# A retention layer and a gated MLP on one core: the same 937 jobs in another order on every engine

## The chip, the cores and the metric

The kernel runs on one core of one Trainium2 chip. The metric is the device time of one execution in microseconds; the time before is the median of three runs. A core has five instruction streams that run on their own and meet at semaphores: PE (TensorE, matrix products, with PEld for its weight loads), DVE (VectorE), ACT (ScalarE), POOL (GpSimd) and SP (SyncE, which here only issues transfers). Each stream is worked off strictly in the order in which it was written. Transfers run on 16 DMA engines that all of SP's queue shares.

## The reference

Inputs are q, k, v of 8 batches x 8 heads x 576 rows x 64, in float32, and the weights of a gated MLP.

```python
scores = scale * q @ k^T                       # per batch and head
ret    = scores * gamma_h ** (t - s), s <= t   # decay, causal
x      = ret @ v, heads side by side           # (8, 576, 512)
h      = gelu(x @ w_in);  u, v = halves of h   # 2 x 512
v_n    = (v - mean) / sqrt(var + 1e-6) * g_ln
v_s    = w_sg @ v_n (over the 576 rows) + b_sg
out    = x + (u * v_s) @ w_out
```

## The kernel before

**Tiles.** Two batches make a pair of 1152 rows, so nine tiles of 128 rows; there are four pairs and 36 tiles (`i` = 0 to 35). The retention of a pair is worked in five blocks `b` (20 in all): blocks 0, 1, 3, 4 of a pair have 256 rows, the one in the middle has 64 rows of each of the two batches. Within a block the causal products are made directly; what came before is carried as a running sum of k^T v ("Z").

**A block's jobs.** SP loads q, k and v (`a_load`, L348; 512 KB each, or q of two blocks at once; the middle block in two transfers of 128 KB each, L351). `a_prep` casts them to bf16 on DVE, ACT or POOL, q and v with the decay multiplied in (L391), k as a plain copy (by the helper `move`, L264 for ACT, L265 for DVE and POOL). PE transposes k and q (`a_Tp` L446, `a_T` L428; blocks 15 and 18 by DMA transpose, `a_TX` L471), and their results are evacuated (`a_Tpev`, `a_Tev`). PE forms the scores (`a_S`, L502), DVE masks them (`a_Sev`, L515, L518), PE forms k^T v (`a_Z`, L538), DVE adds it up (L563, L566) and it is cast (`a_Zev`). PE forms the block's output (`a_O`, `a_O2`, L584), which is evacuated into xT (`a_Oev`).

**A tile's jobs.** V half of the input product (`m_V`, L652), gelu (`m_Vg`, ACT, L659), statistics (`m_stats`, DVE, L667, L668), 1/sqrt (`m_rs`, four POOL instructions, L672 to L675), norm (`m_norm`, ACT, L684, L687); U half (`m_U`, L699) and gelu (`m_Ug`, L709). When a batch's tiles are normalised, eight W products mix its rows (`m_W`, L718: five matmuls each, named by (batch, column block, row half)) and DVE multiplies each with u (`m_Wg`, L728). The output product (`m_O`, L749) is added to x by DVE (`m_Oev`, L766); for tiles from 9 on x comes as a DMA transpose of xT (`m_X`, L758), and `m_store` (L771) writes the tile.

**Weights.** w_in comes in two transfers of 1 MB (V half first, then U half), w_sg in three (L292 twice, L296), w_out in one; each is cast on the way. w_sg is transposed on PE into wT (`build_wT`, L819), evacuated, and shifted by two transfers for the second batch of a pair. Small products turn g_ln and b_sg into columns and rows.

**What sets the order.** Every piece of work is a `Job` with a default engine and, for many, a choice of others (`alt`). Jobs are numbered in the order in which the kernel's loops create them, 0 to 936. The string `ORDER` lists all numbers once; a letter behind a number sets its engine (D, A or P for DVE, ACT, POOL). The kernel emits the jobs in that order, so the string sets at once the sequence on each engine, the engine of the movable jobs, the rotation of the buffers (eight `ld`, three `vb`, two `pp` and four `d` of PSUM, five `xr`, and so on) and what waits for what. The times in the `Job` calls play no part in it.

```python
def follow(self, order):
    for x in order.split():
        if x[0] == "f":
            j = self.fill(int(x[1:]), ...)
        else:
            j = self.jobs[int(x.rstrip("DAP"))]
            if not x.isdigit():
                j.eng = {"D": "DVE", "A": "ACT", "P": "POOL"}[x[-1]]
        self.done.append(j)
```

`fill` puts warm-up matmuls on zeros before the first real work: `f2` one of 256 columns, `f1` one of 128.

Job numbers that are spoken of below:

| number | job |
|---|---|
| 0, 1, 2 | loads of q, k, v of block 0 |
| 3, 9 | loads of w_in, V half and U half; 4, 5 and 10, 11 their casts |
| 12, 13, 14 | loads of q, k, v of block 2; 23 is q of block 3 |
| 15, 16, 17 | loads of w_sg; 18 to 22 their casts |
| 102, 104 | PE transposes of k and q of block 0; 103, 105 their evacuations |
| 108 | cast of v of block 1; 297 is the Z product of block 1 |
| 132, 133, 136 | casts of q of block 5 and its transposes on PE |
| 315, 330, 331 | m_rs of tiles 2 and 4, norm of tile 4 |
| 333 | the first W product |
| 59, 62, 64 | loads of v of blocks 14, 15, 16; 179, 185 the casts of the first two |
| 63, 187 | load and cast of k of block 16; 69 the load of k of block 18 |
| 65, 66, 67 | loads of q, k, v of block 17 |
| 576, 578 | DMA transpose and evacuation of tile 13; 577 its product |
| 585, 586, 587 | output product, evacuation and store of tile 14 |
| 926, 930 | DMA transposes of tiles 34 and 35; 928 is tile 34's evacuation |

Of the kernel before, what the change touches and what calls it, by code (L numbers as in the profile page):

```python
# [20 lines left out]
    '0 f2 1 2 6 7 99D 83D 3 100A 102 8 73 103D 101P 104 74 105A 9 106P 17 203 77 204 12 205 84P 107A 275 206 75 '  # L21
    '277A 109 76D 78D 111 110D 85P 280 112A 5P 281 4A 282D 207 276 283A 278 15 284 108P 208 13 209 285 16 279A 286 '
    '297 287 298 210 11A 10P 14 300 299A 290 23 288 22A 113P 289 301 291 294 80A 302 292 303D 304A 24 18D 305 293 '
    '114D 19A 311 306 313 25 295 307 20P 296 116 79P 308 31 117D 314 21P 115P 211 309 89 212 312 32 310 93 321 94A '
    '118D 322 318 90A 95 324A 33 87 319 315 119A 323D 96D 325 320D 86A 88D 121 34 326 123 120P 328 122A 327 316 '
    '124D 37 329 330 361 215 317 213 362 216 91 35 125P 331 92D 214 333 335 26 363P 126A 127P 366 336 334 128 364 '
    '367 130 368D 369A 339 332 129D 341 131D 365A 350 39 340 219 132P 342 383 217 220 370 36 348 351 371 133P 384 '
    '373 218 337 38 372 134P 136 349 385 137D 138A 386 343 374 387A 140 40 375 81A 389 344 388A 380 141D 98 28 395 '
    '390 338 29 221 223 41 381 222 378 135P 396 376 224 379 30 392 139P 391 97 377 227 27 44 433 397 434 435A 393 '
    '228 142P 382 438 455 436 398 225 143P 394 439 42 352 440A 45 456 441A 399 458 355 437A 226 442 144P 400 356D '  # L30
    '145 353A 43 445 146D 457A 443 448 446 444 401 357 450 150D 412 451 229 447 449 459 417 230 452 408 413 354 418 '
    '410 409 46 147P 479 460 476 480 461D 419 482A 47 453 481D 463 411 454 148P 420 483 478D 464 477 462A 427 82A '
    '149D 466 465 428A 153P 484 429 151 467 485 50 523 155 152D 469 48 156A 154P 486 524 526 402 468 470 488 233 '
    '487 231 234 406 52 404 473 403 235 232 49 345 157P 475 236 358 525A 405 528 359A 407 158D 237 346A 545 529 490 '
    '347 414 238 58 159P 530A 51 471 489 163D 531A 421 415D 472 474 546 161 527D 54 422A 165 162D 532 360 166D 535 '
    '424 60 536 160D 533 547 425A 534 600 56 241 548 537 538 550A 53 602A 601 540 549A 542 242 539 55 557 541 603 '
    '167P 243 558 239 551 240 544 164P 430 552 244 543 57 491 169P 431A 493 554 494 492 61 605 553 555 174P 622 245 '
    '59 606 556 604P 499 607A 507 623 608A 561 625 609 178A 508 500 615 624A 246 168P 610 497 616 64 611 626 562 '
    '172P 498 170 563 627 643 171D 612 628A 515 629D 645A 173P 564 613 559 565 644 416 247 560 175P 511 180 501 '
    '181A 630 423 502 182P 248 503 495 614 631 176 426 632 617 584 183P 496 568 618 63 177D 638 432 67 184P 509 569 '  # L40
    '639 646 510 619 251 62 690 252 647 580 648A 649A 504 691 620 581 692P 516 65 693 179P 505 187A 253 517 249 633 '
# [1087 lines left out]
```

## Time and profile before

| | |
|---|---|
| time before, median of 3 runs | 211.9 us (211.15 to 212.1) |
| the profiled execution, its own time | 212.94 us |
| its span | 211.2 us |
| busy: PE, DVE, ACT, POOL | 187.3, 160.3, 120.5, 101.4 us |
| moved by DMA | 49.04 MB, mean 232 GB/s |
| mean granted clock of PE | 0.992 |

Times in the profile are microseconds from the start of the span. A line of a timeline gives the start, the duration, the engine, the line of the kernel, the operation and its tiles, the count of instructions merged into it, and in brackets the idle time just before it on that engine, with what ended it. A line of stages gives the stretch, its length, then busy time and count of instructions for each engine, the granted clock of PE, the DMA engines' mean busy share and the GB/s moved. PE's ends are modelled, so a busy PE is not PE at its peak. The clock column counts as full any time for which the trace has no record, as before 20.5 us here.

### The profile page before, as it was taken

The numbers are of one execution on the slowest core, as the hardware profiler recorded it, in microseconds if no ns is written. First come the engines' busy times: TensorE is split into PE (matmuls) and PEld (weight loads), VectorE is DVE, ScalarE is ACT, GpSimd is POOL, SyncE is SP. The second block draws the span as 40 slices with busy tenths as digits, with TensorE's granted clock in tenths as the row PEclk, the third lists the DMA queues.
The fourth block names the chain that finished last, engine by engine and source line by source line (L and its number), as shares of the span: only waits on it lengthen the run. The fifth ranks groups of instructions, "written<-read, shape, count | busy, mean of one in ns | idle before, by whom it ended". The sixth has DMA issues, their size and how long they took to land.

```text
span 211.2 us, 7761 instructions
## 1 busy us (share of the span) xinstructions
PE 187.3 (89%) x3313; PEld 127.4 (60%) x3341; DVE 160.3 (76%) x312; ACT 120.5 (57%) x196; POOL 101.4 (48%) x157
## 2 busy tenths in 40 slices
PE   2288787799799999999999988799999999999992
PEld 0265454576575757657667746477567666656661
DVE  5576757799698879998886858897787699665673
ACT  5246695944788386667596444766636653255300
POOL 8266547876664696405689746244236071022000
PEclk9999997999999999999999999999999999999999
DMA  5999999999999999799999699999698966147875
GB/s 163 290 341 281 234 206 291 301 300 291 234 197 289 276 318 257 171 247 334 269 287 227 180 280 159 231 211 180 221 303 157 216 187 202 53 108 204 165 219 204
DMA packets 87109, 49.04 MB, mean 232 GB/s; under 512 B 37082, under 2 KB 80354, under 8 KB 87074
## 3 DMA queue, kind: packets, MB, share of 16 engines
q1 hardware_dynamic: 87056, 48.53, 95.3%
q8 instruction: 26, 0.43, 0.9%
q14 instruction: 9, 0.07, 0.1%
q10 hardware_dynamic: 18, 0.00, 0.0%
HBM read 32.79 MB, written 9.44 MB: 200 GB/s over the span
## 4 chain that ended last, share of the span: by engine, by line
PE 68%; DMA 11%; DVE 6%; SPq 5%; ACT 4%; issue 3%; POOL 2%; DVEq 0%; POOLq 0%
PE wp L718 17%; PE hv L652 12%; PE op L749 12%; PE hu L699 11%; PE pp L584 6%; DMA ld<-in_k_dram 6%; PE pp L502 4%; DMA ld<-in_q_dram 4%; SPq L351 3%; PE pp L428 2%; PE zp L538 2%; DVE ret L515 2%; ACT qT L264 1%; DMA xr<-xT 1%; PE pp L446 1%
## 5 line engine op out<-in xcount | busy, mean ns | idle before, releaser
L515 DVE TENSOR_TENSOR ret<-pp,msk 128x1024 bf16<-128x1024 f32 x32 | 38.6, 1217 | 4.5 <-PE pp L502 4.4
L718 PE MATMUL wp<-wT,vn 128*128 128x288 bf16 x256 | 41.1, 286 | 0.8 <-DVE wT L265 0.8
L699 PE MATMUL hu<-xT,w_in 128*128 128x256 bf16 (+1 forms) x320 | 36.2, 262 | 2.2 <-POOL w_in L265 1.4
L652 PE MATMUL hv<-w_in,xT 128*128 128x512 bf16 x127 | 36.0, 391 | 1.6 <-issue 0.4
L667 DVE BATCH_NORM_STATS2 bst<-vg 128x6 f32<-128x512 f32 x36 | 24.7, 685 | 13.9 <-ACT vg L659 13.9
L749 PE MATMUL op<-w_out,uT 128*128 128x512 bf16 (+1 forms) x137 | 34.4, 373 | 0.8 <-DVE uT L728 0.2
L699 PEld LDWEIGHTS <-w_in 128*128 128x128 bf16 x320 | 28.1, 98 | 9.0 <-POOL w_in L265 1.9
L728 DVE TENSOR_TENSOR uT<-wp,uT 128x288 bf16<-128x288 f32 x64 | 27.5, 448 | 6.8 <-PE wp L718 6.2
L672 POOL TENSOR_SCALAR mv<-mv 128x2 f32<-128x2 f32 (+1 forms) x20 | 5.4, 271 | 56.0 <-DVE mv L668 43.3
L391 POOL TENSOR_TENSOR vb<-ld,gpow 128x1024 bf16<-128x1024 f32 (+1 forms) x16 | 27.8, 1743 | 9.3 <-DMA ld<-in_v_dram 9.2
L687 ACT ACTIVATE vn<-vg,mv 128x512 bf16<-128x512 f32 x32 | 25.3, 807 | 10.3 <-POOL mv L675 10.3
L709 ACT ACTIVATE uT<-hu 128x512 bf16<-128x512 f32 x36 | 20.9, 594 | 15.8 <-PE hu L699 15.7
L718 PEld LDWEIGHTS <-vn 128*128 128x128 bf16 x256 | 24.2, 98 | 9.5 <-ACT vmid L684 1.0
L659 ACT ACTIVATE vg<-hv 128x512 f32<-128x512 f32 x36 | 21.0, 593 | 11.5 <-PE hv L652 5.8
L264 ACT ACTIVATE xT<-pp 128x512 bf16<-128x512 f32 (+1 forms) x31 | 16.6, 566 | 18.3 <-PE pp L584 15.0
L391 POOL TENSOR_TENSOR qb<-ldq,gpow 128x1024 bf16<-128x1024 f32 x11 | 20.7, 1904 | 9.2 <-DMA ldq<-in_q_dram 7.9
L766 DVE TENSOR_TENSOR ob<-op,xr 128x512 f32<-128x512 f32 (+1 forms) x28 | 18.5, 668 | 6.3 <-PE op L749 6.0
L652 PEld LDWEIGHTS <-xT 128*128 128x128 bf16 x144 | 13.5, 100 | 13.4 <-issue 1.3
L749 PEld LDWEIGHTS <-uT 128*128 128x128 bf16 x148 | 14.0, 98 | 11.9 <-issue 0.4
L718 PE MATMUL wp<-wT,vmid 128*128 128x288 bf16 x64 | 18.0, 287 | 0.0
L673 POOL TENSOR_TENSOR mv<-mv,mhalf 128x2 f32<-128x2 f32 (+1 forms) x20 | 13.8, 690 | 1.7
L584 PE MATMUL pp<-qT,zb 64*64 64x128 bf16 (+1 forms) x256 | 12.2, 225 | 1.5 <-issue 1.0
(115 smaller groups left out, 253.6 us busy)
## 6 DMA issues: line engine op xcount, KB each, us to landing
out_dram<-ob SPq DMA_DIRECT2D x35, 256.0 KB, 2.8
ld<-in_k_dram SPq DMA_DIRECT2D x16, 512.0 KB, 6.6
ld<-in_v_dram SPq DMA_DIRECT2D x16, 512.0 KB, 6.8
ldq<-in_q_dram SPq DMA_DIRECT2D x6, 1024.0 KB, 7.7
ld<-in_q_dram SPq DMA_DIRECT2D x4, 512.0 KB, 7.4
xT<-in_moe_w_sg_dram SPq DMA_DIRECT2D x2, 576.0 KB, 8.5
xT<-in_moe_w_in_dram SPq DMA_DIRECT2D x1, 1024.0 KB, 8.3
uT<-in_moe_w_in_dram SPq DMA_DIRECT2D x1, 1024.0 KB
```

The lines of the kernel that those rows point to most:

```text
L391: ve.tensor_tensor(dst, src, g.unsqueeze(len(src.shape) - 1).to_broadcast(list(src.shape)), op=Alu.mult)
L515: ins = nc.vector.tensor_tensor(ret[:].rearrange("p r (k t) -> p (r k) t", k=2), sc[:].rearrange("p r (k t) -> p (r k) t", k=2), (msk2 if ...
L584: nc.tensor.matmul(ot[64 * c:64 * c + 64, bank, j * cs:(j + 1) * cs], lhsT, rhs, start=(bank, c) not in begun, stop=True, skip_group_check ...
L652: ins = nc.tensor.matmul(hv[:], xTs[p][:, m, kk, :], w_in[:, kk, F2:], start=(kk == 0), stop=(kk == KK - 1))
L659: unfence(nc.scalar.activation(vgs[i][:], cur.pop(("hv", i))[:], Act.Gelu_apprx_tanh), ("V", i))
L667: nc.vector.bn_stats(bst[:], vgs[i][:])
L687: nc.scalar.activation(vn[:], vg[:], Act.Identity, scale=mv[:, s, 2:3], bias=mv[:, s, 3:4])
L699: ins = nc.tensor.matmul(hu[:, n, :], w_in[:, kk, 128 * c:128 * c + 128], xTs[p][:, m:m + w, kk, :], start=(kk == 0), stop=(kk == KK - 1), ...
L709: unfence(nc.scalar.activation(uTs[p][:, c0:c1, 128 * m:128 * m + 128 * w], cur.pop(("hu", i, half))[:], Act.Gelu_apprx_tanh), ("U", i, half))
L718: ins = nc.tensor.matmul(ps[:], vns[t0 + j][e][:, 128 * c:128 * c + 128], wT[e][:, j, half * HS:(half + 1) * HS], start=(j == 0), stop=(j ...
L728: ins = nc.vector.tensor_tensor(uTs[p][:, c, col:col + HS], cur.pop(("wp", b, c, half))[:], uTs[p][:, c, col:col + HS], op=Alu.mult)
L749: ins = nc.tensor.matmul(op[:], uTs[p][:, c, r], w_out[:, c, cs], start=(p >= XP and c == 0), stop=(c == KK - 1), skip_group_check=True)
```

## The change

The string `ORDER` is replaced; nothing else differs. The new one holds the same job numbers, `f1` in place of `f2`, other engine letters on 79 jobs, and other positions for most jobs. A job moves by four places on PE on average, by 26 at most. The first 44 PE jobs are the same set in both, and so are the first 190. On SP the load of v of block 0 now comes ahead of that of k, q of block 2 ahead of the U half of w_in, and k, v of block 2 and q of block 3 ahead of w_sg. Of the engines' jobs, 28 go from ACT or DVE to POOL, 15 from POOL to ACT or DVE, 19 from DVE to ACT and 17 from ACT to DVE.

The diff, cut to the lines that hold the head, the places named in the prediction, and the end:

```diff
-    '0 f2 1 2 6 7 99D 83D 3 100A 102 8 73 103D 101P 104 74 105A 9 106P 17 203 77 204 12 205 84P 107A 275 206 75 '
-    '277A 109 76D 78D 111 110D 85P 280 112A 5P 281 4A 282D 207 276 283A 278 15 284 108P 208 13 209 285 16 279A 286 '
-    '297 287 298 210 11A 10P 14 300 299A 290 23 288 22A 113P 289 301 291 294 80A 302 292 303D 304A 24 18D 305 293 '
-    '114D 19A 311 306 313 25 295 307 20P 296 116 79P 308 31 117D 314 21P 115P 211 309 89 212 312 32 310 93 321 94A '
...
-    '172P 498 170 563 627 643 171D 612 628A 515 629D 645A 173P 564 613 559 565 644 416 247 560 175P 511 180 501 '
-    '181A 630 423 502 182P 248 503 495 614 631 176 426 632 617 584 183P 496 568 618 63 177D 638 432 67 184P 509 569 '
-    '639 646 510 619 251 62 690 252 647 580 648A 649A 504 691 620 581 692P 516 65 693 179P 505 187A 253 517 249 633 '
...
-    '847 892 926 872 855 897 744 848 873 849 900 745 904 856 901 902 918 905 898 903 746 850 899 922 914 851 911 '
-    '915 852 906 912 916 907 913 908 917 930 919 909 923 920 931 921 924 934 927 925 935 932 936 928 933 929 '
+    '0 f1 2 1 6 7 99D 73 74 3 101P 8 83P 100A 102 12 104 103D 275 106P 105A 77 276 277A 203 78A 9 75 204 107A 85P '
+    '205 13 206 76A 109 111 112A 278 280 110D 79A 281 5D 282A 4P 283A 14 108D 23 297 113D 209 284 298 300 299P 210 '
+    '207 279P 285 287 81P 208 288 286 17 301 11P 15 289 302 16 10P 24 114A 304A 294 116 25 290 117D 303D 292 291 '
+    '115P 295 31 211 305 212 118P 321 306 308 293 307 311 19A 18P 309 22D 322 318 296 313 310 32 20P 312 323D 314 '
...
+    '540 498 552 553 55 493 541 69 243 168A 494 239 622 543 538 623 244 61 554 539 625 544 495 240 555 430 63 174A '
...
+    '511 180 184A 508 617 614 503 187P 499 618 181D 509 175P 177A 630 500 510 580 619 631 62 646 581 690 251 647 '
+    '691 59 570 648A 252 519 182P 620 512 621 693 426 633 571 632 504 183P 634 513 649A 636 694A 635 249 186 253 '
...
+    '565 255 642 767 712 769D 696 585 697A 768 713 698A 770 699 656 586 256 702 658 703 520 700 587 659 657 65 '
+    '572 521 676 701 66 714 573 257 518 704 715 660 717A 506 677 716A 707 596 709 661 258 705 708 588 197P 710 261 '
...
+    '848 930 833 898 834 849 753 872 754 854 873 899 902 855 904 903 856 900 905 918 850 901 911 851 914 852 912 '
+    '916 913 908 917 922 915 906 909 919 926 907 931 920 934 932 923 921 935 933 927 924 936 925 928 929 '
```

## The prediction

> **What bounds the kernel now.** I read the page first, for the busy shares and the forty slices. Columns of the slices: one digit for 5.3 us, in tenths.
>
> ```profile
> span 211.2 us, 7761 instructions
> PE 187.3 (89%) x3313; PEld 127.4 (60%) x3341; DVE 160.3 (76%) x312; ACT 120.5 (57%) x196; POOL 101.4 (48%) x157
> ...
> PE   2288787799799999999999988799999999999992
> ...
> PEclk9999997999999999999999999999999999999999
> DMA  5999999999999999799999699999698966147875
> ```
>
> TensorE (PE) is busy 187.3 of 211.2 us. Its weak slices are the first eight, two near 125 us and the last; the DMA engines are as full as it until 165 us. Next I cut the span into stages (us; then busy us and count of PE, weight loads, DVE, ACT, POOL; granted clock, DMA share, GB/s).
>
> ```profile
> 0.00:9.00 9.00, 1.77 (x19) 0.96 (x19) 4.69 (x23) 4.21 (x5) 4.45 (x26) 1.00 0.85 215
> 9.00:21.00 12.00, 9.57 (x234) 6.92 (x233) 8.61 (x20) 5.82 (x8) 7.87 (x6) 1.00 1.15 309
> 21.00:42.00 21.00, 15.86 (x297) 10.65 (x299) 14.07 (x29) 16.19 (x27) 13.43 (x20) 0.92 1.13 257
> 42.00:60.00 18.00, 16.53 (x356) 11.59 (x362) 15.73 (x25) 11.02 (x19) 10.88 (x11) 1.00 1.11 266
> 60.00:113.00 53.00, 52.31 (x1140) 36.49 (x1144) 44.83 (x78) 37.22 (x65) 33.40 (x43) 1.00 1.04 268
> 113.00:134.00 21.00, 18.35 (x368) 12.82 (x364) 14.93 (x29) 10.56 (x18) 13.50 (x19) 1.00 1.04 205
> 134.00:200.00 66.00, 65.53 (x883) 43.62 (x892) 51.26 (x99) 35.50 (x59) 17.90 (x34) 1.00 0.81 186
> ```
>
> From 60 to 113 and from 134 to 200 us PE idles 0.69 and 0.47 us: an order can give little there and lose much. What can be won lies before 42 us (14.8 us idle), in 42 to 60 (1.5), in 113 to 134 (2.65) and in the last 4 us.
>
> The head, in order of time:
>
> ```profile
> 7.34 1.06 ACT L264 ACTIVATE qb<-ld 128x1024 bf16<-128x1024 f32 x1 [1.77 <-DMA ld<-in_k_dram]
> 8.45 0.45 PEld L446 LDWEIGHTS <-qb 64*128 64x128 bf16 x16 [6.71 <-ACT qb L264]
> ...
> 9.85 0.61 PE L446 MATMUL pp<-ident,qb 64*128 64x64 bf16 x16 [0.58 <-DVE qT L265]
> ...
> 11.57 0.64 PE L502 MATMUL pp<-qT 64*64 64x128 bf16 x16 [1.11 <-ACT qT L264]
> ```
>
> PE's first real work waits for k of block 0 and its cast; then each step waits for the one before. The third view is the clock, in three neighbouring stretches of 3.4 us:
>
> ```profile
> 27.35:30.76 3.41, 3.36 (x53) 2.10 (x50) 1.79 (x4) 3.22 (x6) 0.51 (x2) 1.00 1.25 204
> 30.76:34.17 3.41, 1.46 (x38) 1.01 (x40) 2.21 (x4) 1.68 (x4) 3.19 (x5) 1.00 0.94 250
> 34.17:37.59 3.42, 3.20 (x39) 1.95 (x36) 2.21 (x6) 2.29 (x5) 2.38 (x5) 0.50 1.17 300
> ```
>
> A stretch in which PE was busy 1.46 of 3.41 us is followed by one at half clock. Last, the dip at 124 to 133 us:
>
> ```profile
> 124.48 1.06 ACT L264 ACTIVATE kb<-ld 128x1024 bf16<-128x1024 f32 x1 [3.09 <-DMA ld<-in_k_dram]
> ...
> 126.77 1.05 PE L699 MATMUL hu<-xT,w_in 128*128 128x128 bf16 x16 [0.74 <-ACT vg L659]
> ...
> 129.41 1.90 POOL L391 TENSOR_TENSOR vb<-ld,gpow 128x1024 bf16<-128x1024 f32 x1
> ...
> 131.37 0.63 PE L538 MATMUL zp<-vb,kb 64*64 64x64 bf16 x44 [0.50 <-POOL vb L391]
> ...
> 133.14 0.25 PE L584 MATMUL pp<-qT,zb 64*64 64x128 bf16 x4 [1.02 <-issue]
> ```
>
> ACT stands 3.09 us for k of block 16, behind it the norm and the gelu that free PE's buffer; the statistics come late, POOL's v cast with them, and PE waits 0.74 and 0.50 us. The 1.02 us are "issue", for which the profile shows no releaser.
>
> **The change, part by part.** It is measured against this execution: 211.2 us of span and 1.7 around it, 212.94, which is 1.04 above the median of 211.9.
>
> *Engines.* 79 jobs change engine. Each at the mean of its kind on its new engine (v cast 1.90 us on POOL, 1.22 on DVE; k cast 1.06 ACT, 1.04 POOL; block evacuation 0.60 ACT, 0.69 DVE): DVE loses 3 us, ACT 4, POOL gains 11. POOL then is at 54%, so this alone is hidden; where a moved job stands behind a late one, it counts below.
>
> *Head to PE's 44th job, the first W product* (both orders hold the same jobs up to there). Loads of 512 KB land every 1.82 us: k of block 0 at 7.32, v at 9.13. After, v is issued first, so k lands at 9.13 and ACT is done at 10.2: 1.8 us later. The two groups of 16 transposes now stand together ahead of the first evacuation, so the 0.58 us wait goes and DVE (0.69) and ACT (1.02) evacuate side by side: scores at 12.6 instead of 11.57. Output of block 0: ACT's casts for block 1 come after one row copy, PE starts it at 16.0 instead of 15.24. Then block 1's v cast, moved from POOL (17.30) to DVE behind a weight cast, is done at 18.8, and the Z product that needs it stands ahead of S and V; at half clock (two V matmuls took 1.06 at 18.91, four took 0.86 at 49.06) V of tile 1 ends at 24.2 instead of 21.8. But before, PE then idled 1.41 us for the U weights, and block 2's q load now runs ahead of that transfer: block 2's scores come at 27.5 instead of 30.18, its output at 28.8 instead of 33.05. The w_sg loads come behind k, v of block 2 and q of block 3; the last lands at about 32.5 instead of 30.4, and two POOL casts (0.67 each) put the build of wT at 33.9. From there k of block 3 (landed 35.03) and the chain v cast, rsqrt, norm (POOL 36.94 to 40.55, ACT to 41.69) rule both orders. W can start at 41.05 if the norm is all it waits for (before: 41.98, after a DVE evacuation at 41.93), or 42.5 if scores, Z and U of block 3 run at half clock. PE's load in the stretch before is 2.15 us by my walk, between 1.46 (half followed) and 2.94 (37.59 to 41.00, full followed). So -0.9 to +0.5. At 50 us both orders meet the transposes of block 5, whose q is cast by POOL from 46.14 to 49.90: that keeps at most 0.5 of a gain. I take -0.3, between the ends.
>
> On the clock, the row is: PE works from 8.45 us and is still at half at 18.91. The Trainium skill ("TensorE: Matmul & The Clock Gate", What you observe) puts the change at about 4 us of sustained matmuls; by that the later start would move the full clock to some 14 us, W would come at 41.05 and the sum fall by 0.2. The trace here does not agree with 4 us: PE waited between groups, and it took 12 us.
>
> *Steady part.* A step from full-array work to 64-row work costs more: after W 0.82 instead of 0.61 us, after V 1.06 instead of 0.77, after U 1.13 instead of 0.89 (starts of PE's jobs). Counted in the two orders, such steps go from 45 to 43: after W 17 to 11 (-1.3 us), V 8 to 12 (+1.2), U 9 to 11 (+0.5), O 6 to 4 (1.17 against 0.77, -0.8), small products the rest (+0.2): -0.2 us, with 0 and -0.5 as ends.
>
> *The dip.* k of block 16 moves from place 65 to 56 on SP, past two loads, three stores and four transposes (k of block 18 now stands ahead of it); its cast goes from ACT to POOL. So ACT's 3.09 us wait goes, and with it the 0.74. If this load were late, POOL would stand with v of block 13 behind it: cast at 111.76 before, needed by PE at 119.35, 5.7 us of slack. v of block 15 moves from place 68 to 65, its cast stands behind v of block 14 (1.90) but follows statistics that come some 3 us earlier: the 0.50 goes too. The issue stall I leave: the same five jobs follow each other there. -1.24; bounds 0 (late by another load) and -2.26 (issue stall too).
>
> *The tail.* The last tile's transpose moves from place 125 to 117 on SP; before, its landing held DVE 0.30 us at 206.46. In its place stands tile 34's at 125, whose evacuation is last: issued by about 205, 2.66 to land as at 203.97, just covered by PE's end at 207.2. -0.25 (0 to -0.4).
>
> The one-matmul-shorter warm-up lies in 6 us of idle PE: nothing.
>
> Sum: -0.3 -0.2 -1.24 -0.25 = -2.0, that is 210.9 from the profiled execution, 209.9 from the median. Late loads may be what made this execution 1.04 slower than the median, so I take the middle: **210.4 us**, 0.7% less.
>
> **Rivals.**
> 1. *The dip stays.* The DMA engines are at 1.04 in 113 to 134, so an earlier place on SP need not mean an earlier landing, and POOL, 11 us fuller, can make v of block 15 as late as before. Against: ACT no longer holds that wait. Then -0.75 of the sum is left: halfway as above, 212.19 and 211.15 give 211.7.
> 2. *Slower by the clock.* Full clock came at 20.5 us, after a stretch with two V matmuls. After, V begins at 20.2, which my walk makes full clock from 23.9. If the small tiles of block 1 do not count, and U waits for weights, it comes two stretches later, at 30.8: 6.8 us at half, 3.4 lost. W starts at 45.4, +3.4, less the 1.7 of the other terms: 213.6. It decides from W at 44.7 (+2.7). Against: PE has V and U to run from 20.2 on. The Trainium skill (same page, What's actually happening) has a window of 3413 ns that runs free of the kernel; the stretches above, 3.41 long, agree, so the phase may differ from run to run.
> 3. *Slower by SP.* The store of tile 14 moves from place 83 to 73; its evacuation follows a PE job at the same place 188 (133.82 to 134.47), so SP stands until 135.5. Behind it, by their rows: q of block 17 2.5 us, k 1.3, two stores 1.1, two transposes 3.2, v 1.9, a store 0.3, a transpose 1.2. So tile 13's transpose is issued at 147 and lands (2.66 as at 203.97, 3.8 on the page) at 149.7 to 150.8, while DVE reaches tile 13's evacuation, moved up from 156.39, at about 148.8. PE goes on with the three O products that follow until 152, four buffers full; one more us late costs PE one. With DMA share 1.21 (130 to 140) it may be 153.5; then PE, DVE and the gelus behind stand 3 us: the forecast's 210.4 plus 3 is 213.4. It decides from 152.7. q of block 17, by the page's 8.2 us, lands at 143.7, is cast by 146 and due at 147.63.
>
> **How the numbers follow.** Forecast 0.46, rival 1 0.22, rival 2 0.17, rival 3 0.15. About 0.5% (1.06 us) is what a measurement can tell here: faster (below 210.84) 0.46, same 0.22, slower 0.32. The forecast's own range is 208.7 (issue stall, step changes and tail at their far ends: -1.02, -0.3, -0.15 from 210.4 make 208.9, and 0.2 of the head's) to 211; the full range goes to rival 2's 213.9, leaving 2 in 10 out.
>
> **What would show it.** PE's first transposes at 10.2 and first scores at 12.6; W at 41 to 42.5; no ACT wait for k of block 16 near 124 and PE idle in 113 to 134 about 1.4; the last DVE evacuation without a wait for a transpose. Wrong if W starts after 44.7, if PE idles over 1 us anywhere from 134 to 200, above all near 150 on DVE's wait for a transpose, or if more than three issue stalls of 1 us appear (before: 31.4, 55.7 and 132.1 us).

## The result, and the profile after

The changed kernel takes 217.72 us (median of 216.21, 216.88, 218.55 and 218.63) where the kernel before took 211.53: ratio 1.029, 95% interval 1.021 to 1.037. It is slower by 6 us; in a second comparison (below) 216.36 against 212.20, ratio 1.025 (1.019 to 1.031). The prediction was 210.4, with 213.9 as the upper end, so size and sign were wrong.

One and the same kernel spreads by several us here (the kernel before: 209.1 to 219.5 in 105 executions), so medians below are over all executions of a run, the ratios to the kernel before (with their 95% intervals, by which a run is judged) leave disturbed executions out, and a profile is one execution.

The page of the changed kernel, from an execution of 216.21 us:

```profile
span 214.5 us, 7790 instructions
PE 189.1 (88%) x3341; PEld 127.2 (59%) x3341; DVE 158.5 (74%) x308; ACT 117.4 (55%) x187; POOL 111.1 (52%) x170
...
PE   1186996759999999999999799999699999999992
...
PEclk9999999997999999999999999999999999999999
DMA  6999999999999990779998999999999963725876
```

Of 5.4 us a slice, PE is weak from 32 to 48 us, the clock dips in the slice after (48 to 54), and there are single weak slices at 118 to 123 and 150 to 155 us. The same stages as before, from 21 us on (us; busy us and count of PE, weight loads, DVE, ACT, POOL; clock, DMA share, GB/s):

```profile
21.00:42.00 21.00, 17.42 (x328) 11.24 (x326) 15.23 (x29) 13.73 (x23) 15.40 (x24) 1.00 1.03 264
42.00:60.00 18.00, 15.36 (x330) 10.49 (x330) 12.55 (x22) 9.38 (x15) 13.45 (x15) 0.91 1.09 262
60.00:113.00 53.00, 52.52 (x1096) 35.98 (x1096) 44.02 (x76) 38.43 (x62) 32.42 (x43) 1.00 0.95 246
113.00:134.00 21.00, 19.55 (x385) 13.72 (x374) 16.75 (x31) 12.34 (x22) 13.45 (x16) 1.00 1.17 223
134.00:200.00 66.00, 64.21 (x933) 41.94 (x925) 48.80 (x95) 32.79 (x54) 25.50 (x45) 1.00 0.91 193
```

Against before, PE idles 1.6 us less in 21 to 42 and 1.2 less in 113 to 134, but 1.2 more in 42 to 60, at a lower clock, and 1.3 more in 134 to 200.

To follow the loss I read from each trace when PE had loaded the last weights of its n-th job, counted behind the warm-up (the prediction counts the warm-up, so its 44th job, the first W product, is the 43rd here). Both orders have done the same jobs after the 43rd, 70th, 187th and last; at 44 and 71 they differ by one job, at 210 and 220 by a few, and all kernels with the new end agree:

| us at PE's job | 44 | 71 | 187 | 210 | 220 | last |
|---|---|---|---|---|---|---|
| before | 42.81 | 60.12 | 134.47 | 148.45 | 155.72 | 206.97 |
| after | 41.76 | 62.30 | 135.47 | 149.79 | 159.01 | 210.25 |
| after, second trace (a0_after) | 40.47 | 62.40 | 134.77 | 149.08 | 158.97 | 210.21 |

So -1.05 us up to job 44, +3.23 from 44 to 71, -1.18 from 71 to 187, +2.28 from 187 on: 3.28 in all (taken where both have done the same jobs: -0.96, +3.06, -1.10 and +2.28). From job 220 to the last both orders take the same 51.2 us, so all of the end's loss lies between 187 and 220.

**The head** went as walked, for what the prediction names:

```profile
9.94 1.04 PE L446 MATMUL pp<-ident,qb 64*128 64x64 bf16 x32 [3.80 <-ACT qb L264]
12.82 0.47 PE L502 MATMUL pp<-qT 64*64 64x128 bf16 x9 [0.64 <-ACT qT L264]
...
40.68 0.65 PE L718 MATMUL wp<-wT,vn 128*128 128x288 bf16 x4
```

Transposes at 9.94 (10.2 was said), scores at 12.82 (12.6), W at 40.68 (41.05).

**42 to 62 us** is where the first loss sits. PE's timeline:

```profile
42.89 0.32 PE L446 MATMUL pp<-ident,qb 64*128 64x64 bf16 x10
44.83 0.26 PE L446 MATMUL pp<-ident,qb 64*128 64x64 bf16 x6 [1.63 <-issue]
...
46.21 0.41 PE L446 MATMUL pp<-ident,qb 64*128 64x64 bf16 x16 [0.88 <-ACT qT L264]
```

PE stops for 1.63 us in the middle of one group of transposes, for nothing that the profile shows, and 0.88 us more for an evacuation. Before, the same two groups ran through:

```profile
43.74 0.41 PE L446 MATMUL pp<-ident,qb 64*128 64x64 bf16 x16
44.07 0.31 PE L584 MATMUL pp<-qT,zb 64*64 64x128 bf16 x8
44.31 0.41 PE L446 MATMUL pp<-ident,qb 64*128 64x64 bf16 x16
```

The two neighbouring clock stretches after:

```profile
44.07:47.48 3.41, 1.77 (x38) 1.42 (x38) 0.76 (x2) 1.82 (x3) 2.73 (x3) 1.00 1.13 293
47.48:50.90 3.42, 3.42 (x58) 2.28 (x57) 2.92 (x6) 0.00 (x0) 3.42 (x4) 0.50 1.08 320
```

With PE busy 1.77 of 3.41 us, the next stretch runs at half clock, and PE is busy all through it: by half of 3.42 us, an estimated 1.7 us of work lost. In the second trace there are two such stretches in a row, from 43.56 to 50.39. Before, the half-clock stretch lay at 34.17, where PE had idle time behind it.

**The dip's** waits for gelu and v cast are gone, but another stall stands just ahead of it, again "issue", inside the Z product of block 13:

```profile
122.31 0.41 PE L538 MATMUL zp<-vb,kb 64*64 64x64 bf16 x28 [1.45 <-issue]
```

**At 152 us** DVE stands at tile 13's evacuation, PE behind it; last, SP's queue:

```profile
152.88 0.69 DVE L766 TENSOR_TENSOR ob<-op,xr 128x512 f32<-128x512 f32 x1 [2.78 <-issue]
```

```profile
153.63 1.02 PE L749 MATMUL op<-w_out,uT 128*128 128x512 bf16 x4 [1.62 <-DVE ob L766]
```

```profile
133.20 3.87 SPq L471 DMA_TRANSPOSE kT<-kb  x1
137.16 0.53 SPq L771 DMA_DIRECT2D out_dram<-ob  x1
137.74 1.69 SPq L351 DMA_DIRECT2D ld<-in_q_dram  x2
...
144.56 1.42 SPq L351 DMA_DIRECT2D ld<-in_v_dram  x2
146.08 0.57 SPq L771 DMA_DIRECT2D out_dram<-ob  x1
146.70 2.55 SPq L758 DMA_TRANSPOSE xr<-xT  x2
```

SP is never free from 133 to 153 us; the pair at 146.70 is the transposes of tiles 16 and 13. The second, tile 13's, was issued from 147.99 to 149.25, and DVE goes on 3.6 us after that. The profile names no releaser for DVE's wait; that it is this transpose is shown by e6_x13 below, which moves this transpose alone ahead and where DVE's wait goes. Before, the DMA engines had room just there:

```profile
145.00:150.00 5.00, 4.95 (x111) 3.45 (x111) 3.54 (x10) 4.28 (x8) 1.45 (x5) 1.00 0.88 269
150.00:155.00 5.00, 4.95 (x56) 2.47 (x55) 4.12 (x8) 1.25 (x3) 0.00 (x0) 1.00 0.69 200
```

and after:

```profile
145.00:150.00 5.00, 5.00 (x112) 3.40 (x111) 4.80 (x9) 2.86 (x6) 3.69 (x5) 1.00 1.38 191
150.00:155.00 5.00, 3.38 (x17) 1.45 (x16) 2.22 (x6) 1.90 (x3) 1.29 (x4) 1.00 1.03 244
```

**The tail** is as predicted: DVE's last evacuations wait for PE (0.41, 0.38 and 0.17 us), not for a transpose.

### The profile page after: what moved, and what is told of

Read it like the earlier page. It is cut to its first block, busy times and chain, and to the rows that moved or that the text cites. A ratio compares the mean times of both kernels' runs of the same rounds, so it can differ in the third digit from the quotient of the medians.

```text
span 214.5 us, 7790 instructions
## 1 busy us (share of the span) xinstructions
PE 189.1 (88%) x3341; PEld 127.2 (59%) x3341; DVE 158.5 (74%) x308; ACT 117.4 (55%) x187; POOL 111.1 (52%) x170
## 4 chain that ended last, share of the span: by engine, by line
PE 76%; DMA 8%; DVE 4%; ACT 4%; issue 3%; POOL 1%; SPq 1%; POOLq 0%; DVEq 0%; ACTq 0%
PE wp L718 18%; PE op L749 14%; PE hv L652 13%; PE hu L699 13%; PE pp L584 6%; DMA ld<-in_v_dram 5%; PE pp L502 5%; DMA ld<-in_k_dram 3%; PE pp L428 3%; PE zp L538 2%; PE pp L446 1%; ACT qT L264 1%; DVE ret L515 1%; PE op L744 1%; ACT qb L264 1%
## 5 line engine op out<-in xcount | busy, mean ns | idle before, releaser
L515 DVE TENSOR_TENSOR ret<-pp,msk 128x1024 bf16<-128x1024 f32 x32 | 38.3, 1217 | 4.9 <-PE pp L502 4.9
L718 PE MATMUL wp<-wT,vn 128*128 128x288 bf16 x256 | 41.6, 290 | 0.0
L652 PE MATMUL hv<-w_in,xT 128*128 128x512 bf16 x144 | 37.8, 389 | 0.1
L749 PE MATMUL op<-w_out,uT 128*128 128x512 bf16 (+1 forms) x148 | 35.7, 374 | 1.6 <-DVE ob L766 1.6
L391 POOL TENSOR_TENSOR vb<-ld,gpow 128x1024 bf16<-128x1024 f32 (+1 forms) x18 | 31.6, 1758 | 8.2 <-DMA ld<-in_v_dram 8.2
L672 POOL TENSOR_SCALAR mv<-mv 128x2 f32<-128x2 f32 (+1 forms) x20 | 4.5, 224 | 53.7 <-DVE mv L668 40.6
L264 ACT ACTIVATE xT<-pp 128x512 bf16<-128x512 f32 (+1 forms) x27 | 14.6, 572 | 12.4 <-PE pp L584 11.2
L391 POOL TENSOR_TENSOR qb<-ldq,gpow 128x1024 bf16<-128x1024 f32 x10 | 18.9, 1906 | 0.7 <-DMA ldq<-in_q_dram 0.7
L265 POOL CAST kb<-ld 128x1024 bf16<-128x1024 f32 x9 | 10.2, 1154 | 5.8 <-DMA ld<-in_k_dram 5.8
```

Source lines behind the costliest of these rows:

```text
L264: return nc.scalar.activation(dst, src, Act.Copy)
L391: ve.tensor_tensor(dst, src, g.unsqueeze(len(src.shape) - 1).to_broadcast(list(src.shape)), op=Alu.mult)
L515: ins = nc.vector.tensor_tensor(ret[:].rearrange("p r (k t) -> p (r k) t", k=2), sc[:].rearrange("p r (k t) -> p (r k) t", k=2), (msk2 if ...
L652: ins = nc.tensor.matmul(hv[:], xTs[p][:, m, kk, :], w_in[:, kk, F2:], start=(kk == 0), stop=(kk == KK - 1))
L718: ins = nc.tensor.matmul(ps[:], vns[t0 + j][e][:, 128 * c:128 * c + 128], wT[e][:, j, half * HS:(half + 1) * HS], start=(j == 0), stop=(j ...
L749: ins = nc.tensor.matmul(op[:], uTs[p][:, c, r], w_out[:, c, cs], start=(p >= XP and c == 0), stop=(c == KK - 1), skip_group_check=True)
```

## The experiments

Theory A: the loss lies in the stalls of 42 to 47 us with their half-clock stretch, and in SP's queue at 152 us. Its rivals came up one by one and stand in the expectations.

### Four stages, each alone

The two strings are cut at a PE job at which both hold the same set, and joined (a job or two moved where a buffer asks for it):

```diff
  e1_head:      new order to PE's 44th job, then old
  e2_mid_back:  new to the 44th, old to the 71st, then new
  e3_end:       old to the 187th, then new
  e4_dip:       old to the 71st, new to the 187th, then old
```

> The new order up to PE's 44th job (the first W product), the old one from there on. Theory A (the loss lies behind the head: in the waits of 43 to 47 us with the half-clock stretch that follows them, and at 152 us): the head itself gains, as the new trace has W 0.96 us earlier, so 210.5 us against 211.5 before. Theory B (the new order of the first loads costs the time, by the later clock and later weights): 213.5 or more.

> The new order with the jobs from PE's 44th to its 71st (about 41 to 61 us) put back into the old order and onto the old engines. Theory A: PE loses 3.1 us there between the two traces (from -0.96 at the 44th job to +2.1 at the 71st), so 214.6 us against 217.7 for the whole change. Theory B, or the theory that the loss is spread evenly over the middle part: 217 to 218.

> The old order up to PE's 187th job (134 us), the new one from there. Theory A: DVE stands for the transpose of tile 13 behind SP's queue, PE behind it, +2.8 us from 134 to 158 in the two traces, 0.5 of it recovered: 213.8 us against 211.5. The rival, that this wait is only there because the new order arrived late: 211.5.

> The old order up to PE's 71st job (61 us), the new one from the 72nd to the 187th (134 us), then the old one. Theory A (the predicted dip step is right): PE's waits of 0.74 and 0.50 us at 126 to 131 go, and 210.4 us against 211.5, if no other stall takes their place; with one issue stall of 1.4 us in it as at 120.9 in the new trace: 211.6. Rival (POOL, 11 us fuller, costs the steady part more than the dip gives): 212.5 or more.

| 10 executions each | median us | the kernel before, same chip | ratio (95% interval) |
|---|---|---|---|
| e1_head | 213.10 | 212.43 | 0.995 (0.990 to 1.0005) |
| e2_mid_back | 213.52 | 212.43 | 1.011 (1.006 to 1.017) |
| e3_end | 212.91 | 212.43 | 1.014 (1.009 to 1.020) |
| e4_dip | 214.57 | 212.43 | 1.012 (1.007 to 1.016) |

The head costs nothing, so theory B is out. Whether it gains the 1 us of theory A stays open: the ratio gives 1.0 us, but its interval reaches just past none, and the medians show no gain. In its trace PE is 1.81 us early at job 44 and 0.29 at job 71.

The stage from 44 to 71 counts: with it put back the ratio is 1.011, where the whole change has 1.025 and 1.029 and the intervals do not meet. That is some 3 us, as theory A says. In e2's trace the stage takes 17.37 us, as before (17.31, against 20.54 with the change); that one execution loses it again later, with a stall of 2.00 us at 120 to 122 us and a half-clock stretch behind it.

The end alone costs 3.0 us by the ratio (0.5 by the medians), where theory A expected 2.3. But not for its reason: in e3's trace jobs 187 to the last take 74.28 us against 72.50, and DVE hardly stands at tile 13's evacuation:

```profile
150.13 0.69 DVE L769 TENSOR_TENSOR ob<-op,xr 128x512 f32<-128x512 f32 x1 [0.23 <-PE op L752]
```

So the rival is right about the wait: without the new order ahead of it, this trace does not have it. In e3 two of the three loads of block 17 go out early, as in the old order, and tile 13's transpose is issued at 144.59, not 147.99. Of the 1.8 us that this trace loses by job 220, 1.08 are a wait of PE for a DVE mask at 143 us.

e4_dip came out as its rival's number says (212.5 or more), but its trace does not show the rival's reason. Jobs 71 to 187 take 73.50 us against 74.35, with the 1.45 us stall in the same Z product, so the step gains 0.85; then old order follows and loses 3.0 us by job 220. The join had put the loads of q, k and v of block 17 at 134 to 139 us on SP, where the old order has two of them at 120 to 125; that this is the cause is not shown, and the run does not isolate the dip.

### The two waits, and the packets of instructions

In the traces so far the longest "issue" stalls inside runs of small matmuls all stood at one place in PE's stream: counting all that PE's trace holds from the start (matmuls, weight loads, and a few semaphore and drain instructions), the first one behind the stall is number 1217, 1729, 4289 or 4801, always 193 modulo 256. The DMA view has a queue that moves 16 KB per packet, and 26 of them make 26 x 256 = 6656 instructions, about all that PE has (the trace has 6699):

```profile
q8 instruction: 26, 0.43, 0.9%
```

That is theory C: PE waits for its next packet of instructions. The edits, each to the changed kernel:

```diff
 e5_tp:   PE's transposes of q (130) ahead of the evacuation of k (129)
-'... 128 367 129A 130 341 131D ...'
+'... 128 367 130 129A 341 131D ...'
 e6_x13:  tile 13's DMA transpose (576) ahead of those of tiles 15, 16
-'... 708 588 197P ... 574 722 576 191P ...'
+'... 708 576 588 197P ... 574 722 191P ...'
 e7_phase: 32 warm-up matmuls (64 instructions) for one (4)
-'0 f1 2 1 ...'
+'0 f64 2 1 ...'
-    warm = consts.tile([128, 256], F32, name="warm")
+    warm = consts.tile([128, 256], BF, name="warm")
-            for w in [256] * (n // 2) + [128] * (n % 2):
+            for w in [16] * (n // 2):
```

> The changed kernel as it is, again, beside the three edits of it below. Expected 217 to 218 us as at its first timing, or lower by what that chip had: the kernel before spread over 209.1 to 216.2 us on the chip of the four runs above.

> The changed kernel with one pair exchanged: PE's transposes of q of block 4 (job 130) are emitted ahead of the evacuation of k's half of the same tile (129), so that they need not wait for it. Theory A (the 0.86 us wait at 45.35 us and the half-clock stretch that follows it cost 0.9 and 1.7 us): 215.1 us where the changed kernel takes 217.7, or 216.8 if only the wait goes. Rival (PE only arrives earlier at the next wait, for W's u or for block 5's q): no change. If the half-clock stretch comes anyway in most executions, from the 1.63 us stall ahead of it alone: 216.8.

> The changed kernel with one transfer moved: the DMA transpose for tile 13 (job 576) goes ahead of those of tiles 15 and 16, the last two transfers of v of block 17 and the store of tile 12 on SP. Theory A: DVE's 2.78 us stand at tile 13's evacuation goes, with it PE's 1.62 us at 152 us: 216 us where the changed kernel takes 217.7. Rival (the backlog on SP only moves to the transposes behind, tiles 15 to 17, or PE is held by something else that late): no change.

> The changed kernel with 60 more PE instructions ahead of its first real work (32 warm-up matmuls of 16 columns in bf16 in place of one of 128 in float32, in time in which PE waits anyway), so that every 16 KB packet of instructions begins 60 instructions earlier in the program. Theory C (PE's issue stalls of 1 to 2 us are waits for the next packet, since in the traces they all lie at the same place modulo 256 instructions): the stalls at 43.2 and 120.9 us go from their places, others may come at other places; between 214.5 and 218 us by where the new ends of packets fall. Rival (they belong to the work at that place, by a semaphore or a buffer): stalls at the same jobs as before, 217.7.

Medians: a0_after 216.36, e5_tp 217.88, e6_x13 216.84, e7_phase 212.95 (12 executions; the others 6), the kernel before 212.20. Ratios: 1.025 (1.019 to 1.031), 1.020 (1.009 to 1.030), 1.022 (1.014 to 1.030) and 1.003 (0.998 to 1.008). Neither wait by itself is worth anything measurable: that these two waits make up the loss is out. The shift is worth some 4 us here. In e5 the 0.88 us are gone, but the stall ahead is 2.16 us there, and two more of 2.07 and 2.28 us follow, each with a half-clock stretch. In e6 the wait only changed hands; ACT's and PE's timelines:

```profile
154.18 1.08 ACT L264 ACTIVATE xT<-pp 128x512 bf16<-128x512 f32 x2 [2.17 <-DMA xr<-xT]
```

```profile
154.84 1.90 PE L652 MATMUL hv<-w_in,xT 128*128 128x512 bf16 x8 [1.76 <-ACT xT L264]
```

The evacuation that refills xT now waits for the transpose that reads it, tile 16's, issued at 148.77. The shift moved the stalls, as theory C says. The same transposes of block 4 that held the 1.63 us now run through, and the 0.88 us stays:

```profile
44.51 0.41 PE L446 MATMUL pp<-ident,qb 64*128 64x64 bf16 x16
44.85 0.31 PE L584 MATMUL pp<-qT,zb 64*64 64x128 bf16 x8
46.04 0.41 PE L446 MATMUL pp<-ident,qb 64*128 64x64 bf16 x16 [0.88 <-ACT qT L264]
```

The trace times of three unshifted and two shifted kernels (read from the packets' transfers and PE's instructions; number of the first instruction behind the stall):

```
kernel      number  mod 256  packet's transfer   PE stands          length
after        1217     193      42.30-43.32      43.20-44.83          1.63
after        4289     193     119.97-120.94    120.86-122.31         1.44
a0_after     1217     193      41.82-42.88      41.92-44.37          2.44
e6_x13       1217     193      42.83-43.91      42.45-45.58          3.13
e7_phase     1729     193      53.92-55.10      55.46-56.67          1.21
e7_phase     2241     193      68.75-69.91      69.92-71.35          1.44
e8_after76   1473     193      45.54-46.73      47.08-48.16          1.08
```

Over the 19 traces other than that of the kernel before (where some matmuls' records are missing) there are 60 stalls over 0.3 us at that place, and each ends 1.2 to 1.8 us after the transfer of a packet ended. At none of the 476 places where a packet of these traces ends and the next begins does PE go on sooner than 1.2 us after the next one's transfer. Apart from one at the very start of e6_x13, no other stall over 0.3 us is an "issue" one. The kernel before obeys too: counted by its weight loads, its stalls of 1.08 us at 55.70 and 1.02 at 132.12 end at numbers 1729 and 4801, 1.62 and 1.37 us after a packet's transfer.

Why the stall at 43 us is new can be read in the same way. PE reached number 961, where the packet before begins, at 38.96 us before and 39.09 after. The next packet's transfer began at 40.20 before and at 42.30 after, and PE ran through its 256 instructions in 4.9 us before and 4.1 after. So the packet came 2.1 us later and PE was 0.8 us quicker; what held the packet's transfer is not shown.

The warm-up matmuls took 0.9 us near 1.1 to 2.0 us, and PE's first transposes stood at 9.71, against 9.94 and 9.74 unshifted, so the shift changes little else in the head.

### Other shifts

To use theory C for numbers I assumed that a packet is asked for when PE enters the one before; in the unshifted trace its transfer starts 1.3 us before that to 6.4 us after. The shift is again made by the count of warm-up matmuls alone (e11_fixed76: with the edits of e5 and e6):

```diff
 e8_after76    -'0 f1 ...'   +'0 f80 ...'
 e9_after180   -'0 f1 ...'   +'0 f184 ...'
 e10_before108 -'0 f2 ...'   +'0 f112 ...'   (the old order)
```

> The changed kernel with 76 more PE instructions ahead of its first real work (40 warm-up matmuls of 16 columns). Theory C: a packet of 256 instructions is fetched once PE has entered the one before it, 0 to 7 us late by the DMA queues, and PE stands if it is through its 256 earlier. From the times of the instructions in the traces I add up, for each shift, what PE comes too early at each end of a packet: 5.1 to 6.8 us for no shift, 3.0 for 60, 1.6 for 76, which is the least. So 1.4 us below the kernel shifted by 60: 211.5 us. Rival (the gain of the shift by 60 came from the extra warm-up matmuls, or by chance): 213 to 216.

> The changed kernel with 180 more PE instructions (92 such matmuls). Theory C: the same sum is 7.6 us here, the most, so 217 to 218.5 us, no better than unshifted (216.4 to 217.7), although it has the most warm-up. Rival (warm-up matmuls help by themselves): 213 or less.

> The kernel before with 108 more PE instructions (56 such matmuls). Theory C: the sum is 7.6 us for the kernel before as it stands and 5.0 with this shift, so 209.6 us against 212.2. Rival (packets matter to the new order alone, since the kernel before shows only one or two issue stalls): 212.

> The changed kernel shifted by 76 as above, with both edits that alone did nothing measurable: PE's transposes of q of block 4 ahead of the evacuation of k's half, and tile 13's DMA transpose ahead of those of tiles 15 and 16. Theory C and theory A together (behind a stall of 2 to 3 us the two waits are hidden, without it they count, 0.86 and 1.5 us): 209.5 us. Rival (the waits are hidden anyway): 211.5, as shifted alone.

Medians 216.50, 218.39, 213.19 and 215.79, the kernel before 213.15 there; ratios 1.018 (1.013 to 1.024), 1.026 (1.018 to 1.033), 0.997 (0.993 to 1.002) and 1.012 (1.006 to 1.018). The second came as said, and shows that warm-up by itself does not help. The others missed, and the shifted kernel before takes the time of the unshifted one, as its rival said: my sum of earliness does not predict the time. In e8_after76 the stage from 44 to 71 does shrink (18.47 us, against 20.54 and 21.93 unshifted), but three more packets are late (0.83, 1.06 and 1.51 us), jobs 71 to 187 take 75.48 us instead of 73.17, and the last job is at 210.18, as unshifted. Four of its six executions ran at a granted clock of 0.998 or more and took 215.9 to 217.6 us, so the full clock alone is not the gain of the shift by 60.

### The end, the dip, and the shift again

```diff
 e12_x16 (changed kernel): transposes of tiles 16 (592) and 13 (576)
-'... 708 588 197P ... 725 592 720 ... 722 576 191P ...'
+'... 708 592 576 588 197P ... 725 720 ... 722 191P ...'
 e13_k16 (kernel before): load of k of block 16 (63), its cast (187)
-'... 628A 515 629D ... 618 63 177D ... 505 187A ...'
+'... 628A 63 515 629D ... 618 177D ... 505 187P ...'
 e14_all60:     e7 with the edits of e5 and e12
 e15_phase60b:  e7 once more
```

> The changed kernel with two transfers moved: the DMA transposes for tiles 16 and 13 (jobs 592, 576) go ahead of that of tile 15, the last part of v of block 17 and the store of tile 12. Moving tile 13's alone left ACT's evacuation into xT standing for tile 16's. Theory D (from 134 us to the end every trace of the new order takes 74.8 to 76.7 us where the old takes 72.5, because SP is behind with transposes at 147 to 152 us): PE's 210th to 220th job take 7.3 to 7.8 us again, and 214.7 us where the changed kernel took 216.4. Rival (SP stays behind as a whole and the next transpose is late): 216.4.

> The kernel before with the dip's step alone: the load of k of block 16 (job 63) moves on SP from place 65 to 57, ahead of five transposes and three stores, and its cast (187) goes to POOL. By the prediction's term PE's waits of 0.74 and 0.50 us near 126 and 131 us go: 211.0 us where the kernel before took 212.2. Rival (with the 1.2 us earlier PE runs into its next packet of instructions, or POOL is late with v of block 15): 212.2 or more.

> The changed kernel with all three: 60 more PE instructions in front, PE's transposes of q of block 4 ahead of k's evacuation, and the transposes for tiles 16 and 13 early. If the three costs add up (stalls for packets with the half-clock stretch behind them, 0.86 us of wait, 1.9 us at 152 us): 210.2 us, below the kernel before by 2. Rival (each fix moves PE on to the next packet or transfer that is late, or the gain of the shift by 60 was chance): 213 to 216.

> The changed kernel with 60 more PE instructions in front, the same as an earlier run, once more. Seven of its twelve executions had 211.0 to 214.1 us and a granted clock of 1.00, which no unshifted execution had, and the one that was profiled was among the others (217.1). Theory C: the median is again 213 or so, and the profile, if it is of such an execution, shows neither a half-clock stretch nor a stall of over 1 us at 42 to 47 us. Rival (chance, or that chip): 216 to 217.

Medians 217.19 (6 executions), 212.72 (12), 213.17 (12) and 215.15 (10), the kernel before 212.13; ratios 1.014 (1.003 to 1.025), 1.000 (0.995 to 1.005), 1.006 (1.001 to 1.011) and 1.006 (1.000 to 1.012).

e12_x16: jobs 210 to 220 take 7.45 us, as theory D says (9.22 before the edit), and DVE's wait for a transpose is gone:

```profile
149.95 0.69 DVE L766 TENSOR_TENSOR ob<-op,xr 128x512 f32<-128x512 f32 x1 [0.22 <-PE op L749]
```

Jobs 187 to the last still take 74.59 us against 74.78 and 75.44. Most of the gain is given back by job 260: PE idles 1.4 us in small waits between 158 and 183 us, where a0_after idles 0.1; the one of them over 0.4 us is for a DMA transpose of q at 171. The median did not follow; the ratio, from three executions, can't tell the 214.7 us that were expected from no change.

e13_k16: the mechanism is right, the gain does not reach the end. In its trace PE is 2.53 us ahead at job 187 (131.94) and 0.84 at the last. Two lines of its PE timeline show what took its place:

```profile
130.02 0.63 PE L538 MATMUL zp<-vb,kb 64*64 64x64 bf16 x44 [1.08 <-POOL vb L391]
...
167.55 0.64 PE L502 MATMUL pp<-qT,kT 64*64 64x128 bf16 x32 [1.07 <-DMA qT<-qb]
```

The 0.50 us for v of block 15 became 1.08, and the DMA transpose of q of block 18 holds an earlier PE at 167 us. The time is that of the kernel before.

e14_all60 missed its 210.2 us and lies in its rival's 213 to 216; the three edits together do not beat the kernel before. e15_phase60b gives less of a gain than e7, in between what theory C and the rival said; its profiled execution, of 217.11 us, shows nothing of the gain.

### Once more the dip and the shift

e16_k16s60 is e13 with the shift of 60, e17_phase60c is e7 a third time.

> The kernel before with the dip's step (k of block 16 loaded earlier, cast on POOL) and 60 more PE instructions in front. The trace of the dip's step alone had PE 2.5 us earlier at its 187th job and lost 1.04 us again at the end of a packet at 166 us. Theory C: with the packets' ends elsewhere that stall goes, 211.3 us against 212.1 before, if no end of a packet falls worse. Rival (every order of this work meets about two such stalls, wherever the ends fall): 212.5.

> The changed kernel with 60 more PE instructions in front a third time, for a profile of an execution at full clock. Theory C: no stall at the first packet's end behind 42 us (it was 1.6 to 3.1 us in every unshifted trace) and no half-clock stretch after it, PE's 71st job at 60 us or before; the whole 211 to 213 us. If that job is at 62 us again, the execution is slow by another cause.

Medians 214.97 (6 executions) and 216.24 (2), the kernel before 211.92; ratios 1.015 (1.009 to 1.022) and 1.023 (1.017 to 1.030). The premise of the first was wrong: the 1.04 us at 166 us in e13 are the DMA transpose shown above, not a packet. With the shift it met packets of 1.22 and 1.49 us at 50 and 57 us and, by a granted clock of 0.96 to 0.984, half-clock stretches in five of six executions; it is slower. In e17 theory C's signs came (at the first packet's end behind 42 us PE stands 0.33 us, and no half-clock stretch follows) and its time did not: job 71 comes at 60.80 and job 187 at 132.95, 1.5 us ahead of the kernel before, and it is as slow as ever. DVE, then PE:

```profile
151.00 0.69 DVE L766 TENSOR_TENSOR ob<-op,xr 128x512 f32<-128x512 f32 x1 [3.42 <-issue]
```

```profile
151.74 1.77 PE L749 MATMUL op<-w_out,uT 128*128 128x512 bf16 x4 [2.25 <-DVE ob L766]
```

The idle time is followed by a half-clock stretch at 151.88. Put side by side, these are the traces that have the new order from job 71 on, with the transposes of tiles 13 and 16 where the change has them:

| us at PE's job | 187 | 210 | 220 | last |
|---|---|---|---|---|
| e17_phase60c | 132.95 | 147.27 | 158.81 | 210.05 |
| a0_after | 134.77 | 149.08 | 158.97 | 210.21 |
| e9_after180 | 135.16 | 149.48 | 158.71 | 210.21 |
| after | 135.47 | 149.79 | 159.01 | 210.25 |
| e8_after76 | 135.50 | 149.82 | 158.94 | 210.18 |
| e15_phase60b | 135.94 | 150.25 | 159.57 | 210.81 |
| e7_phase | 136.26 | 150.58 | 159.67 | 210.91 |
| e2_mid_back | 136.65 | 150.96 | 160.05 | 211.29 |
| e5_tp | 138.82 | 153.13 | 160.58 | 211.81 |

From a0_after down to e7_phase job 210 varies by 1.5 us and job 220 by 1.0, and in all six DVE goes on between 152.59 and 153.55; in e5_tp PE comes later and DVE waits only 0.24. With both transposes moved (e12_x16, e14_all60) the ten jobs take 7.45 us in place of 9.1 to 9.9. So in these six profiles the transposes, behind SP's queue, set job 220. e17_phase60c is no proof of it: there SP was 1.6 us earlier and DVE went on at 151.00, and the half-clock stretch took that back, which is chance.

What the shift of 60 is worth: its 24 executions (e7, e15, e17) have a median of 214.5 us, the ten of the changed kernel as it is 216.7. 14 of the 24 had a granted clock of at least 0.996, with a median of 212.3; of the ten, none. None of those 14 was among the four profiled (e14's included), so what they save at the end isn't shown. No version tried beats the kernel before.

## Why the prediction was wrong

- *Head.* Right in the trace (the first W product's last weights 0.96 us earlier; -0.9 was the lower end). What of it is kept in the time can't be told: e1_head's ratio is 0.995 (0.990 to 1.0005). Rival 2 did not happen: full clock came at 23.59 us (23.9 was walked), W at 40.68.
- *From job 44 to 71.* Here the sum failed. The prediction let both orders meet at block 5's transposes near 50 us and gave the stretch no cost. Measured: +3.23 and +4.62 us in the two traces of the changed kernel, and some 3 us in the time when the stage is put back (e2). What the traces show in it is a late packet (1.63 and 2.44 us), the order of jobs 129 and 130 (0.88 and 0.72), which I had in front of me and did not walk, and a half-clock stretch moved from where PE had idle time to where it had none (an estimated 1.7, and twice that in the second trace). That the stage costs the time is shown; how its cost splits among these is not: taking away the wait of job 129 alone gained nothing measurable (e5), and e8's shorter stage did not shorten the whole.
- *"The issue stall I leave: the same five jobs follow each other there."* Wrong in kind. Such a stall does not belong to jobs; it belongs to a place modulo 256 in PE's stream, to a late packet, and to how quickly PE is through the 256 instructions ahead. The stall at 132 us went and one of 1.45 us came at 121. Of the three stalls that the prediction lists for the kernel before, the one at 31.4 us is none of them: PE waits there 1.18 us for POOL's cast of w_sg.
- *The dip.* The mechanism is right: ACT no longer waits for k of block 16, and jobs 165 to 187 take 12.9 us instead of 15.2. The term -1.24 was taken as a gain at the end, and that failed: e13 has PE 2.53 us ahead behind the dip, and nothing in the time. In its trace 0.84 us are left at the end, and one wait behind the dip, for a DMA transpose, took 1.07.
- *Rival 3* was the right mechanism for the loss at the end, at 0.15. I let SP start at 135.5 and land tile 13's transpose at 149.7 to 150.8, under the 152.7 from which it decides. Store 14 went out at 137.16, as the transpose of k of block 15 ahead of it held SP to 137.1, and tile 13's issue began at 147.99, one us later than walked. From there DVE took 4.9 us to go on, at 152.88, where the prediction had 2.66 to 3.8 for the landing. Its three us are 2.28 here, of 3.28 in this pair of traces, and 1.62 of them are PE's wait; about 0.5 us of the rest is there without it too (187 to 220 takes 21.76 us in e12 and 21.25 before).
- *Steady part and tail* cannot be told from the noise; the tail's wait is gone as said.
- *A slip in the sums.* Rival 2's 213.6 is counted from the median alone, the forecast and the other rivals from halfway between it and the profiled execution; by that it would be 214.1, and the range's 213.9 is neither. The measured 217.72 is above all three.

What stays open: how the 4 to 6 us split in executions without a profile. By the ratios the head gives -1.0 us, the stage from 44 to 71 some 3 to 4, e4's stage +2.5 and the end +3.0, which is more than the whole; but e4's holds the displaced loads of block 17, and the two traces of the changed kernel are only 3.3 us behind that of the kernel before.

## What to carry to other kernels

Where PE is 90% busy and the transfers are close behind, a wait removed in the middle may be worth nothing (e5, e6 and e13): show first that no transfer further on sets the time, and look for a job whose time does not move when PE comes earlier. An order can have a cost that no job owns, the instruction packets; find the stalls' number modulo 256 before explaining them by the work at that place, and try another offset before judging an order (one offset gained 2.2 us in the median here, others nothing). A half-clock stretch costs an estimated 1.7 us only where PE is busy in it, so an order can lose by moving one.

## What the runs showed of the hardware

- PE waits for instructions: 0.3 to 3.1 us, always at the same number modulo 256, and it goes on 1.2 to 1.8 us after a packet's transfer has ended, in 60 cases in 19 traces. The Trainium skill ("Runtime: NRT & Kernel Launch", Instruction fetch mechanics) says that instructions come in blocks of 16 KiB, 256 each, and that crossing a boundary is mostly hidden. The traces agree on the block and not on the hiding: in the changed kernel's first trace, with DMA engines at a share near 1, a packet's transfer started up to 6.4 us after PE had entered the one before.
- The clock goes to half for a stretch of 3.41 us when PE was busy for about half of the stretch before. From 30 us to PE's end, the traces have such stretches after 0.50 to 2.10 us of PE work, and full ones after no less than 1.65. The Trainium skill ("TensorE: Matmul & The Clock Gate", What's actually happening) names an idle window as the condition; here PE needed only to be idle for about half of one.
- A DMA transpose that reads a buffer holds the engine that refills it: with one of two late transposes moved ahead, DVE's wait of 2.78 us went and ACT's of 2.17 us came.
